# A decode layer on one core: TensorE's program becomes a loop of four turns, K is turned with each head's columns side by side, and w1 is loaded behind wq

## The chip, the core and the metric

The kernel runs on one core of a Trainium2 chip. The core has five engines, each with its own instruction stream: TensorE (matrix products, PE in the profile), VectorE (DVE), ScalarE (ACT), GpSimd (POOL) and SyncE (SP), which here only issues transfers. Sixteen DMA engines move data between the chip's HBM and the on-chip memory SBUF; products land in PSUM. The engines wait for each other by semaphores. The metric is the device time of one execution in microseconds; the median of three runs is given.

## What is computed

One decode step for two sequences (B = 2, one token each): a layer norm of x, then attention over the last 2048 positions of a cache with 8 K/V heads of 256 and 16 query heads, and beside it a small feed-forward gate.

```python
xn = _layernorm(x)                                    # x: 2 x 1 x 448
q  = (xn @ wq).reshape(B, 1, 16, 256)                 # wq: 448 x 4096
k, v = k_cache[:, :, Sk-W:], v_cache[:, :, Sk-W:]     # 2 x 8 x 2048 x 256 each
p  = softmax(einsum("bhqd,bhkd->bhqk", q, repeat(k, 2)) * 256**-0.5)
s  = einsum("bhqk,bhkd->bhqd", p, repeat(v, 2)).reshape(B, 1, 4096) @ wo
g  = silu(relu(xn @ w1) @ w2)                         # w1: 448 x 1792, w2: 1792 x 448
out = x + s * g
```

All tensors are bf16. K and V are 16.8 MB each, wq and wo 3.7 MB each, w1 and w2 1.6 MB each: 44.1 MB are read and 1.8 KB written.

## The kernel before

**Units.** The attention is cut into four units u (`NU`), each of one sequence and four K/V heads: 4 MB of K and 4 MB of V. A transfer lays a unit out with 32 blocks of positions by four heads over the 128 partitions, 64 positions of 256 elements in each. For each unit the following steps run.

- `do_T` (T): VectorE turns K, 32 x 32 words at a time, from `kbuf` into `kt`, in four transposes of 128 x 2048 words. A word is a pair of bf16 elements. There are two `kt` buffers, for even and odd units, and a transpose writes in the order in which it reads.
- `do_S` (S): 32 products of TensorE give the scores, four at a time in four column tiles of the array, one for each head. The moving operand is `kt`, read with a step of 8 elements (16 bytes). The stationary one is a strip of `q_big`, made once for all units by four copies of VectorE behind the turn of q.
- `ch_max`, `ch_spread`, `ch_pt`: VectorE takes the maximum (`mx`, `mxt`, `nbt`, `nb`), ScalarE the exponential with its sum, TensorE spreads the result over the partitions with 16 products and sums, VectorE masks it into `pt` and takes the reciprocal of the sum.
- `do_PV` (PV): 32 products with V as the moving operand, four at a time; ScalarE copies the result to `o_sb`.
- `do_o_pe`, `do_at_exp`, `do_at`: small products and two VectorE steps that lay the unit's result out in `at2`.

**The rest.** Ahead of the units come the layer norm and `do_q`, 28 products against wq. The feed-forward part is `do_h` (first layer, with `do_hn`, `do_hT` and `do_hs`: clamp, turn, copy, on VectorE and TensorE) and `do_F` (second layer, 14 products). At the end come `fold_sums` and `do_gate` for the gate, and 32 blocks of the product with wo, of which the first `WO_TILED` = 24 run in column tiles of the whole width; a copy and four products fold these into one sum, and the other 8, cut in four each, are added to it. Two VectorE steps and a store close the program.

**Order.** Nothing is planned by a machine: `op` and `dma` append to one list per engine, and `run` emits each list as straight code, with a wait in front of an instruction for what it depends on and hasn't yet waited for. So the order in the source from line 466 on is the order on each engine, and a waiting instruction holds everything behind it on its engine. All large transfers are issued by SP in one order: wq, K(0), K(1), V(0), K(2) when T(0) is done, K(3) after T(1), V(1) after PV(0), V(2) after T(2) (into `kbuf[0]`), w1 after S(2) (into a `kt` buffer), V(3) after PV(1), w2, and wo in five parts after T(3).

On TensorE and VectorE the units overlap: T(u+1) lies beside S(u), its last quarter beside the exponential, and the small products of unit u lie between those of unit u+1. The lines that matter most below:

```python
            deps = [d_k[u], st.get(("S", u - 2))] + ([st["q_mm"]] if u == 1 else [])
            st["T", u] = pr.op(DVE, lambda e: e.transpose(
                dst[:, 2048 * c:2048 * c + 2048], src[:, 2048 * c:2048 * c + 2048]), deps)
...
                    o = pr.op(PE, mm(sbk[u % 2][32 * h:32 * h + 8, :], q_big[:, lo:lo + 8],
                                     view(kt[u % 2], 64 * (gp // 2) + gp % 2 + 2 * h, [[256, TS], [8, 8]]),
                                     gp == 0, gp == NG - 1, tile_position=(0, 32 * h)), deps)
```

Every product goes through the helper `mm`, so nearly all of TensorE's work has its line, 187, and the groups are told apart by their tiles: `sp<-kt,q_big` is S, `sp<-e_sb,sel` the spread, `sp<-vbuf,pt` and `sp<-kbuf,pt` are PV, `gbk<-kbuf,at` and `hbk<-kbuf,at` the product with wo. Transposes of K have line 315, all transfers line 37.

Of the kernel before, what the change touches and what calls it, by code (L numbers as in the profile page):

```python
# [15 lines left out]
class _Op:  # L16
    __slots__ = ("eng", "fn", "deps", "dma", "needed", "value", "sem")

    def __init__(self, eng, fn, deps, dma):
        self.eng, self.fn, self.deps, self.dma = eng, fn, deps, dma  # L20
        self.needed, self.value, self.sem = dma, 0, None


class _Prog:


    def __init__(self, nc, es):
        self.nc, self.es = nc, es
        self.lists = {PE: [], DVE: [], ACTE: [], SP: [], POOL: []}

    def op(self, eng, fn, deps=()):
        o = _Op(eng, fn, [d for d in deps if d is not None], False)
        self.lists[eng].append(o)
        return o

    def dma(self, eng, dst, src, deps=()):
        o = _Op(eng, lambda e: e.dma_start(dst, src), [d for d in deps if d is not None], True)
        self.lists[eng].append(o)
        return o

    def run(self):

        nc = self.nc
        n = 0
        for ops in self.lists.values():
            for o in ops:
                for d in o.deps:
                    d.needed = True
        for e, ops in self.lists.items():
            sem, count = self.es.enter_context(self.nc.semaphore(f"s_{e}")), 0  # L50
            for o in ops:
                if o.dma:
                    n += 1
                    o.sem, o.value = self.es.enter_context(self.nc.semaphore(f"d_{n}")), 16
                elif o.needed:
                    count += 1
                    o.sem, o.value = sem, count
        engines = ((POOL, nc.gpsimd), (SP, nc.sync), (ACTE, nc.scalar), (PE, nc.tensor), (DVE, nc.vector))
        for name, eng in engines:
            hint = eng.mark_branch_hint_location() if name == DVE else None  # L60
            self.emit(eng, self.lists[name])
            if hint is not None:
                eng.br("fin").branch_hint(hint)
        nc.switch_bb("fin")

    def emit(self, eng, ops):
        seen = {}
        for o in ops:
# [9 lines left out]
            if o.needed:  # L78
                made.then_inc(o.sem, 16 if o.dma else 1)


def bass_recurrent_scan__sliding_block_cached__dense_activation_relu__decode_kernel(
# [30 lines left out]
    WO_PARTS = [10, 10, 4, 6, 2]  # L113
    WO_TILED = 24

    es = contextlib.ExitStack()
    with es:
# [31 lines left out]
        q_big = named("q_big", [128, NU * NG * 32], BF)  # L149
# [10 lines left out]
        nb = [named(f"nb{i}", [128, 32], F32) for i in range(2)]  # L160
        ssum = [named(f"ssum{i}", [128, 1], F32) for i in range(2)]
        rs = [named(f"rs{i}", [128, 1], F32) for i in range(NU)]
        e_sb = [named(f"e_sb{i}", [128, 512], BF) for i in range(2)]
        pt = [named(f"pt{i}", [128, 512], BF) for i in range(2)]
        fs = named("fs", [128, D], F32)
        o_sb = named("o_sb", [128, 512], BF)
        at_exp = named("at_exp", [128, 64], BF)
# [3 lines left out]
        kt = [named(f"kt{i}", [128, UW], BF) for i in range(2)]  # L171
        wq_sb = kt[1]
        wo_sb = kbuf[1]
        w1_sb = kt[0]
        W2_AT = SLOTS * FC

        sp = psum("sp", [128, 2048], F32)
        sbk = [sp[:, 512 * i:512 * i + 512] for i in range(2)]
# [17 lines left out]

        def unit_src(u, cache):
# [13 lines left out]
        vhome = [vbuf, vbuf, kbuf[0], vbuf]  # L211
        d_k, d_v = {}, {}
# [7 lines left out]
        p_qb = pr.op(POOL, lambda e: e.memset(q_big[:, :].bitcast(F32), 0.0))  # L220
# [6 lines left out]
        a_z = [pr.op(ACTE, lambda e, t=t: e.memzero(t[:, :])) for t in (mbk, gbk, hbk)]  # L227
# [45 lines left out]
        for r in range(1, 4):  # L273
            v_xr = pr.op(DVE, lambda e, r=r: e.tensor_copy(
                view(xr, 32 * r, [[128, SLOTS], [1, 4]]), view(xr, 0, [[128, SLOTS], [1, 4]])), [v_xr])
# [6 lines left out]
        def load_v(u, deps=()):  # L282
            d_v[u] = pr.dma(SP, vhome[u][:, :], unit_src(u, A_v_cache), deps)


        def do_q():
# [19 lines left out]
            for qd in range(4):  # L306
                st["q"] = pr.op(DVE, lambda e, qd=qd: e.tensor_copy(  # L307
                    view(q_big, qd, [[NG * 32, NU], [32, NG], [4, 8]], n=32, p0=32 * qd),
                    view(q_t, 0, [[1, NU], [32, NG], [256, 8]], n=32, p0=32 * qd)), [v, p_qb])


        def do_T(u, c):
            src, dst = kbuf[u % 2][:, :].bitcast(F32), kt[u % 2][:, :].bitcast(F32)
            deps = [d_k[u], st.get(("S", u - 2))] + ([st["q_mm"]] if u == 1 else [])
            st["T", u] = pr.op(DVE, lambda e: e.transpose(  # L315
                dst[:, 2048 * c:2048 * c + 2048], src[:, 2048 * c:2048 * c + 2048]), deps)

        def do_S(u):
            deps = [st["T", u], st["q"], st.get(("exp", u - 2)), *st["q_n"]]
            for gp in range(NG):  # L320
                for h in range(HU):
                    lo = (u * NG + gp) * 32 + 8 * h
                    o = pr.op(PE, mm(sbk[u % 2][32 * h:32 * h + 8, :], q_big[:, lo:lo + 8],
                                     view(kt[u % 2], 64 * (gp // 2) + gp % 2 + 2 * h, [[256, TS], [8, 8]]),
                                     gp == 0, gp == NG - 1, tile_position=(0, 32 * h)), deps)
                    deps = []
            st["S", u] = o


        def ch_max(u):  # L330
            k = u % 2
            v = pr.op(DVE, lambda e: e.tensor_reduce(out=mx[:, 0:1], in_=sbk[k], axis=AX.X, op=ALU.max),  # L332
                      [st["S", u], p_mx, st.get("mxt")])
            v = st["mxt"] = pr.op(DVE, lambda e: e.transpose(mxt[:, :], mx[:, :]), [v, st.get("neg")])  # L334
            v = st["neg"] = pr.op(DVE, lambda e: e.tensor_reduce(
                out=view(nbt, 0, [[4, 2], [1, 4]]), in_=view(mxt, 0, [[4, 2], [0, 4], [1, 4]]),
                axis=AX.X, op=ALU.max, negate=True), [v, p_nbt, st.get("nb")])
            v = st["nb"] = pr.op(DVE, lambda e: e.transpose(nb[k][:, :], nbt[:, :]), [v, st.get(("exp", u - 2))])  # L338
            st["exp", u] = pr.op(ACTE, lambda e: e.activation(  # L339
                e_sb[k][:, :], sbk[k], ACT.Exp,  # L340
                bias=nb[k][:, 0:1], accum_out=ssum[k][:, 0:1]),
                [v, st.get(("spread", u - 2)), st.get(("sum", u - 2))])

        def ch_spread(u):
            deps = [st["exp", u], v_sel, st.get(("pt", u - 1)), *st["q_n"]]
            for i in range(16):
                r, kb = divmod(i, 8)
                o = pr.op(PE, mm(spk[:, TS * r:TS * r + TS], sel[:, 128 * i:128 * i + 128],
                                 view(e_sb[u % 2], kb, [[8, TS]]), i == 0, kb == 7), deps)
                deps = []  # L350
            st["spread", u] = o
            st["sum", u] = pr.op(PE, mm(view(xbk, u, [[1, 1]]), sumsel[:, :], ssum[u % 2][:, 0:1], True, True),
                                 [v_ss, st.get(("r", u - 1))])

        def ch_pt(u):
            st["pt", u] = pr.op(DVE, lambda e: e.tensor_tensor(  # L356
                out=view(pt[u % 2], 0, [[128, 4], [1, 128]]), in0=view(sp, 1024, [[0, 4], [1, 128]]),
                in1=view(hmask, 0, [[1, 4], [0, 128]]), op=ALU.mult),
                [st["spread", u], v_hm, st.get(("PV", u - 2))])
# [221 lines left out]
```

## Time and profile before

| | |
|---|---|
| median of 3 runs | 111.37 us (111.21 to 111.9) |
| profiled execution: its time, its span | 111.33 us, 109.9 us |
| TensorE products, busy | 68.5 us (62% of the span) |
| VectorE, busy | 59.8 us (54%) |
| ScalarE, GpSimd, busy | 12.2 us, 4.4 us |
| mean granted clock of TensorE | 0.81 |
| HBM read | 44.11 MB, 402 GB/s over the span |

The span reaches from the first to the last instruction. In the row PEclk the digits are the clock granted to TensorE in tenths of full speed (9 is 90% or more), in the row DMA the busy share of the sixteen DMA engines, each digit for a fortieth of the span (2.75 us). A line of the groups has the source line, engine, operation, output and inputs, partitions x elements of each and the number of instructions; then the busy time in us and the mean ns of one; then the idle time ahead of them with what ended it.

### The profile page before, as it was taken

To read this page: it belongs to the slowest core of one execution; us is meant where nothing else is said; L and a number is where in the kernel's file an instruction comes from. 1 tells how busy PE (TensorE), PEld (TensorE's weight loads), DVE (VectorE), ACT (ScalarE), POOL (GpSimd) and SP (SyncE) were. 2 spreads that over 40 slices of the span, in tenths; PEclk is the share of its full clock that TensorE was granted. 3 is DMA by queue.
4 is the path that set the end of the run, shared out by engine and by line. 5 is a ranking of instruction groups with operands and counts; after the bars stand their busy time and mean duration, and the time that the engine had idled before them with its cause. 6 is when DMAs were issued, how large, how long until landed. Compare 5 with 4: busy or idle time off the path is not lost.

```text
span 109.9 us, 1131 instructions
## 1 busy us (share of the span) xinstructions
PE 68.5 (62%) x490; PEld 23.3 (21%) x469; DVE 59.8 (54%) x84; ACT 12.2 (11%) x21; POOL 4.4 (4%) x14
## 2 busy tenths in 40 slices
PE   0010699500001995579995699989999892556871
PEld 0000001000000110553110622146213841211330
DVE  2167000399999996825984879995005026003621
ACT  2930000340000000201000200040001300020000
POOL 7800000000000000000000000000000000000000
PEclk9999999995555599656999755999999999955555
DMA  6798998999899989989999999999899998999920
GB/s 168 334 460 388 513 430 382 418 489 430 382 501 441 394 382 525 430 382 406 483 430 394 430 489 406 394 477 447 344 425 496 453 406 363 413 433 417 413 115 1
DMA packets 2463, 44.16 MB, mean 402 GB/s; under 512 B 282, under 2 KB 412, under 8 KB 924
## 3 DMA queue, kind: packets, MB, share of 16 engines
q1 hardware_dynamic: 2432, 44.11, 94.3%
q8 instruction: 3, 0.05, 0.2%
q10 hardware_dynamic: 28, 0.01, 0.0%
HBM read 44.11 MB, written 0.00 MB: 402 GB/s over the span
## 4 chain that ended last, share of the span: by engine, by line
DMA 36%; PE 32%; DVE 26%; issue 2%; ACT 1%; SPq 0%
DMA kbuf<-in_A_wo_dram 26%; PE sp L187 23%; DVE kt L315 15%; DMA kt<-in_A_wq_dram 10%; PE sp L192 6%; DVE q_t L305 2%; DVE mx L332 2%; DVE q_big L307 2%; PE gbk L187 2%; ACT e_sb L339 1%; PE hbk L187 1%; DVE q_n L299 1%; DVE pt L356 1%; DVE mxt L334 1%; DVE nb L338 1%
## 5 line engine op out<-in xcount | busy, mean ns | idle before, releaser
L187 PE MATMUL sp<-kt,q_big 128*8 128x512 bf16 x128 | 30.1, 1088 | 14.4 <-DVE kt L315 14.4
L315 DVE STREAM_TRANSPOSE kt<-kbuf 128x2048 f32<-128x2048 f32 x16 | 35.6, 2274 | 2.8 <-DMA kbuf<-in_A_k_cache_dram 2.7
L187 PEld LDWEIGHTS sp<-kt,q_big 128*8 128x8 bf16 x128 | 4.7, 103 | 34.0 <-issue 18.4
L187 PE MATMUL sp<-e_sb,sel 128*128 128x64 bf16 x64 | 8.1, 294 | 5.3 <-ACT e_sb L339 5.3
L187 PE MATMUL sp<-vbuf,pt 128*16 128x512 bf16 x96 | 8.0, 492 | 2.4 <-DMA vbuf<-in_A_v_cache_dram 1.9
L187 PEld LDWEIGHTS sp<-e_sb,sel 128*128 128x128 bf16 x64 | 7.0, 119 | 8.2 <-ACT e_sb L339 8.2
L339 ACT ACTIVATE e_sb<-sp,nb 128x512 bf16<-128x512 f32 x4 | 2.8, 688 | 51.5 <-DVE nb L338 51.5
L332 DVE TENSOR_REDUCE mx<-sp 128x1 f32<-128x512 f32 x4 | 2.7, 687 | 9.4 <-PE sp L187 9.4
L192 PE MATMUL sp<-kt,xr 128*128 128x512 bf16 x21 | 7.7, 488 | 0.0
L299 DVE TENSOR_SCALAR q_n<-sp 128x1024 bf16<-128x1024 f32 x1 | 1.2, 1225 | 10.5 <-PE sp L192 10.5
L187 PE MATMUL sp<-kt,xr 128*128 128x512 bf16 x7 | 3.6, 512 | 3.7 <-DMA kt<-in_A_wq_dram 3.7
L187 PE MATMUL mbk<-ident,xg 2*128 2x2 bf16 x7 | 0.3, 163 | 7.9 <-DVE xg L237 7.9
L356 DVE TENSOR_TENSOR pt<-sp,hmask 128x512 bf16<-128x512 f32 x4 | 2.8, 698 | 4.2 <-PE sp L187 4.2
L387 DVE TENSOR_TENSOR at_exp<-mbk,qmask 128x64 bf16<-128x64 f32 x4 | 0.8, 204 | 7.2 <-PE mbk L187 7.2
L187 PEld LDWEIGHTS sp<-vbuf,pt 128*16 128x16 bf16 x96 | 3.1, 120 | 7.0 <-DMA vbuf<-in_A_v_cache_dram 3.7
L372 ACT ACTIVATE o_sb<-sp 128x512 bf16<-128x512 f32 x4 | 2.4, 593 | 17.9 <-PE sp L187 17.9
L399 DVE TENSOR_SCALAR at<-mbk,rs 64x32 bf16<-64x32 f32 x4 | 1.4, 350 | 3.6 <-PE mbk L187 3.6
L187 PEld LDWEIGHTS sp<-kt,xr 128*128 128x128 bf16 x7 | 0.8, 121 | 10.7 <-issue 6.9
L187 PE MATMUL gbk<-kbuf,at 128*17 128x448 bf16 x24 | 3.0, 570 | 0.1
L302 ACT ACTIVATE q_n<-sp 128x1024 bf16<-128x1024 f32 x1 | 1.0, 1024 | 14.5 <-PE sp L192 14.5
L187 PE MATMUL gbk<-kt,h_sb 128*17 128x448 bf16 x14 | 1.7, 569 | 1.3 <-DMA kt<-in_B_w_dram 1.3
L305 DVE STREAM_TRANSPOSE q_t<-q_n 128x2048 bf16<-128x2048 bf16 x1 | 2.3, 2311 | 0.0
(74 smaller groups left out, 45.8 us busy)
## 6 DMA issues: line engine op xcount, KB each, us to landing
kbuf<-in_A_k_cache_dram SPq DMA_DIRECT2D x4, 4096.0 KB, 17.9
vbuf<-in_A_v_cache_dram SPq DMA_DIRECT2D x3, 4096.0 KB, 21.6
kbuf<-in_A_v_cache_dram SPq DMA_DIRECT2D x1, 4096.0 KB, 18.7
kt<-in_A_wq_dram SPq DMA_DIRECT2D x1, 3584.0 KB, 11.2
kt<-in_B_w_dram SPq DMA_DIRECT2D x2, 1568.0 KB, 19.3
kbuf<-in_A_wo_dram SPq DMA_DIRECT2D x2, 1120.0 KB, 27.3
kbuf<-in_A_wo_dram SPq DMA_DIRECT2D x1, 672.0 KB, 29.3
kbuf<-in_A_wo_dram SPq DMA_DIRECT2D x1, 448.0 KB, 29.1
```

The lines of the kernel that those rows point to most:

```text
L187: return lambda e: e.matmul(out_ap, lhsT=lhsT, rhs=rhs, start=start, stop=stop, skip_group_check=True, **kw)
L192: return lambda e: e.add_instruction(mybir.InstMatmult(name=nc.get_next_instruction_name(), start_tensor_calc=start, stop_tensor_calc=stop ...
L299: e.tensor_scalar(out=view(q_n, 0, [[64, 16], [32, 2], [1, 32]]), in0=view(sp, 0, [[64, 16], [1, 2], [2, 32]]), scalar1=SCALE, scalar2=Non ...
L305: v = pr.op(DVE, lambda e: e.transpose(q_t[:, :], q_n[:, :]), halves)
L307: st["q"] = pr.op(DVE, lambda e, qd=qd: e.tensor_copy(view(q_big, qd, [[NG * 32, NU], [32, NG], [4, 8]], n=32, p0=32 * qd), view(q_t, 0, [ ...
L315: st["T", u] = pr.op(DVE, lambda e: e.transpose(dst[:, 2048 * c:2048 * c + 2048], src[:, 2048 * c:2048 * c + 2048]), deps)
L332: v = pr.op(DVE, lambda e: e.tensor_reduce(out=mx[:, 0:1], in_=sbk[k], axis=AX.X, op=ALU.max), [st["S", u], p_mx, st.get("mxt")])
L334: v = st["mxt"] = pr.op(DVE, lambda e: e.transpose(mxt[:, :], mx[:, :]), [v, st.get("neg")])
L339: st["exp", u] = pr.op(ACTE, lambda e: e.activation(e_sb[k][:, :], sbk[k], ACT.Exp, bias=nb[k][:, 0:1], accum_out=ssum[k][:, 0:1]), [v, st ...
L356: st["pt", u] = pr.op(DVE, lambda e: e.tensor_tensor(out=view(pt[u % 2], 0, [[128, 4], [1, 128]]), in0=view(sp, 1024, [[0, 4], [1, 128]]), ...
L372: st["osb", u] = pr.op(ACTE, lambda e: e.activation(o_sb[:, :], obk[:, :], ACT.Copy), [o, st.get(("oT", u - 1))])
L399: st["at", u] = st["mbk"] = pr.op(DVE, lambda e: e.tensor_scalar(out=view(at2, 16 * b, [[32, 32]], n=64, p0=p0), in0=mbk[p0:p0 + 64, 32:64 ...
```

## The change

- **TensorE.** Straight code up to the first layer of the feed-forward part, then a loop of four turns, one for each unit, then straight code for the end. A turn is S, (in the last turn: the second layer), spread, PV, the products on `o_sb` and the last small one. The loop waits on semaphores of its own, one per kind of step, against a register that counts the turns (`r`; `v16` for transfers, whose semaphores rise by 16).
- **One buffer of each.** For the loop's addresses to be the same in each turn, `kt`, `pt`, `e_sb`, `nb`, `ssum` and the score bank are single, and V always goes to `vbuf`. T(u+1) waits for S(u).
- **T.** Each transpose now writes its words so that a head's columns lie together: word (b, k, h) goes to h * 2048 + b * 8 + k, so that neighbouring writes are 8 KB apart. S then reads `kt` with a step of 2 elements (4 bytes).
- **The q strips.** `q_big` goes; four ScalarE copies fill `qb` for each unit.
- **Transfers.** w1 follows wq, into `vbuf`; V(0) waits for the first layer's products, V(1) for PV(0), K(3) follows it. V(2) and V(3) come in two halves, each waiting for the half of PV that reads it; w2 lies between them, in wq's place. wo comes last, into `kbuf[0]`, in parts of 10, 12, 6, 2 and 2 blocks for 10, 10, 4, 6 and 2, and 28 blocks are tiled for 24.
- **First layer.** Runs right behind q, with 128 columns of the stationary operand instead of 4 and each loaded once for two products; its clamps and copy go from VectorE to ScalarE.
- **Small steps.** `at_exp` has 128 columns for 64, and its product writes all partitions.

```diff
-    WO_PARTS = [10, 10, 4, 6, 2]
-    WO_TILED = 24
+    WO_PARTS = [10, 12, 6, 2, 2]
+    WO_TILED = 28
...
-        kt = [named(f"kt{i}", [128, UW], BF) for i in range(2)]
-        wq_sb = kt[1]
-        wo_sb = kbuf[1]
-        w1_sb = kt[0]
+        kt = named("kt", [128, UW], BF)
+        wf = named("wf", [128, UW], BF)
+        wq_sb, w2_sb, w1_sb = wf, wf, vbuf
+        wo_sb = kbuf[0]
...
+        def load_v_half(u, k):
+            lo, hi = k * UW // 2, (k + 1) * UW // 2
+            pr.dma(SP, vbuf[:, lo:hi], unit_src(u, A_v_cache)[:, :, lo:hi],
+                   [st["PV" if k else "PVa", u - 1]], kind="VB" if k else "VA")
...
         def do_T(u, c):
-            src, dst = kbuf[u % 2][:, :].bitcast(F32), kt[u % 2][:, :].bitcast(F32)
-            deps = [d_k[u], st.get(("S", u - 2))] + ([st["q_mm"]] if u == 1 else [])
+            src, dst = kbuf[u % 2][:, :].bitcast(F32), kt[:, :].bitcast(F32)
             st["T", u] = pr.op(DVE, lambda e: e.transpose(
-                dst[:, 2048 * c:2048 * c + 2048], src[:, 2048 * c:2048 * c + 2048]), deps)
+                dst.rearrange("p (h b k) -> p b k h", h=HU, k=8)[:, 64 * c:64 * c + 64],
+                src[:, 2048 * c:2048 * c + 2048].rearrange("p (b k h) -> p b k h", k=8, h=HU)), [d_k[u], st.get(("S", u - 1))],
+                kind="T" if c == 3 else None)
...
+        def do_qb(u):
+            for qd in range(4):
+                st["qb", u] = pr.op(ACTE, lambda e, qd=qd: e.activation(
+                    view(qb, qd, [[32, NG], [4, 8]], n=32, p0=32 * qd),
+                    view(q_t, u, [[32, NG], [256, 8]], n=32, p0=32 * qd), ACT.Copy),
+                    [st["q"], p_qb, st.get(("S", u - 1))], kind="QB" if qd == 3 else None)
...
+            with block("turn"):
+                wait("QB", r)
+                wait("T", r)
+                for gp in range(NG):
+                    for h in range(HU):
+                        o = mm(sbk[32 * h:32 * h + 8, :], qb[:, 32 * gp + 8 * h:32 * gp + 8 * h + 8],
+                               view(kt, 4096 * h + 16 * (gp // 2) + gp % 2, [[64, TS], [2, 8]]),
+                               gp == 0, gp == NG - 1, tile_position=(0, 32 * h))(pe)
+                o.then_inc(pr.kinds["S"], 1)
+                pe.br_lt(r, NU, on_true="spread", on_false="second_layer")
+            with block("second_layer"):
+                do_F(pe)
+                pe.br("spread")
+            with block("spread"):
+                hint = pe.mark_branch_hint_location()
+                wait("EXP", r)
...
+                wait("PT", r)
+                for k in range(2):
+                    wait("VB" if k else "VA", v16)
+                    for tp in range(16):
...
+                    o.then_inc(pr.kinds["PV" if k else "PVa"], 1)
+                wait("OSB", r)
+                wait("AT", r)
...
+                wait("AE", r)
+                mm(mbk[:, 32:64], at_exp[:, :], fold[:, :], False, True)(pe).then_inc(pr.kinds["at_mm"], 1)
+                pe.reg_add(r, r, 1)
+                pe.reg_add(v16, v16, 16)
+                pe.br_lt(r, NU + 1, on_true="turn", on_false="tail").branch_hint(hint)
...
+        d_w1 = pr.dma(SP, w1_sb[:, 0:SLOTS * FC], w1_src)
         load_k(0)
         load_k(1)
         do_q()
+        do_h()
...
+        do_qb(0)
         for c in range(4):
             do_T(0, c)
...
+        load_v(0, [st["h", 0], st["h", 1]])
         load_k(2, [st["T", 0]])
...
+        for u in range(NU):
+            ch_max(u)
+            ch_exp(u)
+            if u < NU - 1:
+                do_qb(u + 1)
+                do_T(u + 1, 0)
+            else:
+                copy_sums(st["F"])
+            ch_pt(u)
+            if u < NU - 1:
+                for c in range(1, 4):
+                    do_T(u + 1, c)
+            do_osb(u)
+            do_at_exp(u)
+            do_at(u)
+            if u == 0:
+                load_v(1)
+                load_k(3, [st["T", 1]])
+        load_v_half(2, 0)
+        load_v_half(2, 1)
+        pr.dma(SP, w2_sb[:, 0:14 * D].rearrange("p (hf f) -> p hf f", hf=2), w2_src, [st["q_mm"]], kind="w2")
+        load_v_half(3, 0)
+        load_v_half(3, 1)
...
-            d_wo[j0] = pr.dma(SP, wo_sb[:, j0 * D:(j0 + n) * D], wo_src[:, j0 * D:(j0 + n) * D], [st["T", 3]])
+            d_wo[j0] = pr.dma(SP, wo_sb[:, j0 * D:(j0 + n) * D], wo_src[:, j0 * D:(j0 + n) * D], [st["T", 2]])
```

## The prediction

> **What bounds the kernel now.** I read the page's 40 slices and its read total first, then the chain, then the groups by line.
>
> ```profile
> PEclk9999999995555599656999755999999999955555
> DMA  6798998999899989989999999999899998999920
> HBM read 44.11 MB, written 0.00 MB: 402 GB/s over the span
> ```
>
> The sixteen DMA engines are busy from the second slice to the thirty-eighth (a slice is 2.75 us), whatever the compute engines do. The page's chain says the same of its end: from 75.26 to 103.75 us it is the transfer of wo, and only 6 us follow. So the kernel is a stream of 44.11 MB at some 427 GB/s (44.11 MB over the 103 us in which it runs). As long as compute keeps ahead of the stream it costs nothing; what decides is whether it still does.
>
> VectorE's and TensorE's groups, with the time of one instruction behind the busy time:
>
> ```profile
> L315 DVE STREAM_TRANSPOSE kt<-kbuf 128x2048 f32<-128x2048 f32 x16 | 35.6, 2274 | 2.8 <-DMA kbuf<-in_A_k_cache_dram 2.7
> L187 PE MATMUL sp<-kt,q_big 128*8 128x512 bf16 x128 | 30.1, 1088 | 14.4 <-DVE kt L315 14.4
> L187 PE MATMUL sp<-kbuf,pt 128*16 128x512 bf16 x32 | 1.9, 382 | 0.0
> ```
>
> Both matmul groups run four at a time. Reading kt in steps of 16 bytes, 32 of them (one unit's scores, S) take 7.50 us; reading V in one run, 32 take 1.93 us, or 3.62 us in the first unit, where the clock was halved (48.00 to 51.62). Four transposes (T, one unit's turn of K) follow one another every 2.22 us: 26.35 to 35.25. Today T of the next unit lies beside S of this one, because kt has two buffers.
>
> **The change, part by part.**
>
> *One kt buffer.* T(u+1) now waits for S(u), and S(u+1) for T(u+1): they add up instead of overlapping. This makes the cost of each decide.
>
> *S.* [...] The reductions on VectorE show what steps cost on a read: one run, 8-byte steps, 64-byte steps.
>
> ```profile
> L246 DVE TENSOR_REDUCE qmask<-ident 128x4 f32<-128x128 bf16 x1 | 0.3, 276 | 0.0
> L253 DVE TENSOR_REDUCE hmask<-ident 128x4 f32<-128x128 bf16 x1 | 0.3, 274 | 0.0
> L251 DVE TENSOR_REDUCE fold<-ident 128x32 bf16<-128x128 bf16 x1 | 0.4, 353 | 0.0
> ```
>
> Steps of 8 bytes are free, so I price S like PV's one run: 1.93 us at full clock, 3.62 at half. Bound above: 7.50 as now. Which clock? TensorE is idle for some 6 us before each S.
>
> ```profile
> 37.00:38.00 1.00, 1.00 (x11) 0.17 (x7) 1.00 (x2) 0.00 (x0) 0.00 (x0) 0.54 0.91 393
> 38.00:39.00 1.00, 1.00 (x12) 0.25 (x8) 1.00 (x1) 0.00 (x0) 0.00 (x0) 1.00 1.06 459
> ```
>
> In these windows (the third number from the right is the granted clock) S(0), begun at 35.29, got the full clock only 2.7 us in. I take 3.62.
>
> *T.* Each transpose now writes its elements 8 KB apart: four heads, then back to the neighbouring word. No row shows such a 4-byte write. From below: free, 2.22 us. From above, the isolated 2-byte writes of the kernel, against one that writes short runs:
>
> ```profile
> L270 DVE TENSOR_TENSOR xr<-mbk,par 128x28 bf16<-128x28 f32 x1 | 0.2, 178 | 0.0
> L432 DVE CAST h_sb<-hbk 128x28 bf16<-128x28 f32 x1 | 0.3, 285 | 0.6 <-PE hbk L187 0.6
> L399 DVE TENSOR_SCALAR at<-mbk,rs 64x32 bf16<-64x32 f32 x4 | 1.4, 350 | 3.6 <-PE mbk L187 3.6
> ```
>
> (285 - 178)/28 is 3.8 ns more for each write, the other row some 5.3; at 3.8, T would take 2.22 + 2048 x 0.0038 = 10 us. [...] Nearest in order is L251: it too visits four places 64 bytes apart and returns to the neighbour of the first; (353 - 276)/128 = 0.60 ns an element, though on a read. I take it: T every 2.22 + 1.23 = 3.45 us. This is the weakest number here, and it counts sixteen times.
>
> [...]
>
> *Start.* w1 (1.6 MB) goes ahead of K(0): 1.6/0.427 = 3.8 us later for everything behind it. K(2) landed at 50.65 (T(2) waited for it) with 20.4 MB in the queue up to it; 9.5 MB are now queued up to K(0), so it lands at 50.65 - 10.9/0.427, about 25.1. T(0) began at 26.35 behind the four copies into q_big (1.82 us), which go to ScalarE; so it begins at 25.2 instead, 1.1 earlier. The first layer (h) runs behind q on TensorE (2.8 us, 87.7 to 90.5 now) from 20.9, its clamps and the q copies on ScalarE; done by about 28, beside T(0). If that cover went, 3 us would be added once.
>
> *SP's queue.* V(0) waits for h (24), K(2) for T(0), V(1) for PV(0), K(3) behind V(1) for T(1), V(2) and V(3) in halves for PV, wo behind all for PV(2). If compute keeps up, each wait ends before the queue is dry (PV(0) 48.5 against some 52, PV(2) 86 against 90.8), and the stream stays whole. The extra issues (three, 0.54 us each) hide behind transfers of 4.9 us. If compute is late the stream has gaps, which cost nothing while compute is later still.
>
> *A turn,* from one S to the next: S 3.62; max to nb 1.44 (42.82 to 44.26); first transpose 3.45, which covers exponential and spread (0.79 + 2.1); pt and reciprocal 0.79; three transposes 10.35; at_exp, its matmul and hand-overs 0.52. PV (3.62, V landed in time), o_sb and its matmuls (0.9) lie beside the three transposes, and are the next thing late if those shrink: 6.66 at the old price still cover them. Sum 20.17.
>
> *The sum.* T(0) ends 25.2 + 13.8 = 39.0; S(3) starts at 39.0 + 3 x 20.17 = 99.5. Last turn: S 3.62, second layer 1.7 (98.46 to 100.1 now), spread 2.1, pt 0.8, PV 1.93 (TensorE has been busy 7 us, so full clock), o_sb 0.62, then 0.27, 0.23, 0.25, 0.4 as now: 111.4. wo has landed by then (PV(2) begins at 88.6, its halves free V's at 90.4 and 92.2; two halves of 4.9 us and wo's 8.6 follow, to about 111). The end: 28 tiled wo products 1.5 (half as fast at half clock), copy 0.68, fold 0.33, sixteen products 0.5 (thirty-two took 0.97), the last two VectorE steps 0.64, store 1.74 (108.16 to 109.9): 116.8. Around the span lie 111.33 - 109.9 = 1.43 us; this execution stands at the median (111.37). That gives 118.2; register, branch and wait instructions of the loop, a few tenths a turn that no row prices (below: nothing), I put at 0.8 in all. **119.0 us.**
>
> Its own range: with T at 3.1 instead of 3.45, 16 x 0.35 = 5.6 less; with PV and wo at half clock 3.3 more, and T at 3.7 four more: 113.5 to 126.
>
> **Rivals.**
>
> *A, scattered writes are free (0.22).* Then T(0) ends at 34.1, S(3) follows T(3), PV(3) follows V's last half at 97.7, and the end is the wo stream again. For it: the transposes keep 1.04 ns an element, and the copies into q_big step 512 bytes at 443 ns for 256. Price: the tail. wo's last tiled piece ends 0.46 MB later in the stream (1.07 us), has six products for four (+0.12), sixteen untiled fewer (-0.47): +0.6, so 111.9, not slower by more than 1%. It decides below a T of about 3.0, where the chain (16 us for each 1 us of T) falls under the stream.
>
> *B, scattered writes are dearer.* At two cycles an element (2.08 ns), T is 4.36 and the sum 16 x 0.91 = 14.6 more: 133.6 (0.08). At the 3.8 ns of L432 it is 7.8 - 1.2 = 6.6 more sixteen times, 224 (0.06).
>
> *C, S is not faster.* The 4-byte step is no run; at 7.50 us, four times 3.9 more: 134.5 (0.06). Against it speaks L253.
>
> *D, the branch back refetches.* The jump stands between one turn's last matmul and the next S. The shortest transfer of the trace, x_sb, took 1.34 us from issue to use (0.74 to 2.08); if each of three jumps costs that, 4 more: 123.0 (0.08). For it: today's program has no jump in TensorE. [...]
>
> **The numbers.** Forecast 0.50. Within 1% is what a measurement of this kernel can hardly tell from no change (its runs span 0.6%). A gives 0.04 faster, 0.16 same, 0.02 slower; of the forecast 0.04 falls to same and 0.01 to faster where T is near 3.0. So faster 0.05, same 0.20, slower 0.75. The range 110.6 to 130 holds A, the forecast and D, some 0.8 of the chance; B and C lie above it.
>
> **What would show it.** The mean of the transpose group: 3.5 us (forecast), 2.27 (A), 4.4 or 10 (B). S per unit: 3.6 or less, else 7.5. DMA slices well below 9 after the half if compute is late; all 9 if A. The chain: transposes and S in turns to the end, not wo. An idle stretch on TensorE ahead of each S with T already done would be D. The forecast is wrong first of all if a read's price does not carry over to a write.

## The result, and the profile after

The changed kernel takes **124.05 us** (median of 4 runs, 123.08 to 124.84) where the kernel before, run beside it, takes 111.29 (110.88 to 111.9): a ratio of 1.114 [1.102, 1.125]. The forecast was 119.0 with a range of 110.6 to 130.0. Here and below, ratios and intervals are taken from runs within 1.5% of the fastest run of the same kernel; where there are too few of them, all runs are listed.

The profiled execution took 123.08 us, with a span of 120.7. Its granted clock, its DMA slices (3.02 us each), its read total and the shares of its chain of waits:

```profile
PEclk9999999995555555555555555555555555596898
DMA  5998989898989999999898989999902799999300
HBM read 44.11 MB, written 0.00 MB: 365 GB/s over the span
DVE 47%; DMA 20%; PE 18%; issue 11%; ACT 1%; SPq 1%
```

The same 44.11 MB are read, but the stream is no longer whole. In slices 30 and 31 it is all but dry (no more was asked for until PV(2), which starts at 90.12 us, had read half of V(2)), and it is over well before the end. VectorE and TensorE now take turns as the bound. The groups by line show what their instructions cost (the last column is idle time ahead of them and what ended it):

```profile
L351 DVE STREAM_TRANSPOSE kt<-kbuf 128x2048 f32<-128x2048 f32 x16 | 57.5, 3684 | 1.0 <-DMA kbuf<-in_A_k_cache_dram 1.0
L221 PE MATMUL sp<-kt,qb 128*8 128x512 bf16 x128 | 14.3, 623 | 15.7 <-DVE kt L351 14.9
L221 PE MATMUL sp<-vbuf,pt 128*16 128x512 bf16 x128 | 14.1, 618 | 3.7 <-DVE pt L380 3.7
L221 PE MATMUL mbk<-fold,at_exp 128*128 128x32 bf16 x4 | 0.8, 203 | 19.2 <-DVE at_exp L392 19.2
```

A transpose went from 2274 to 3684 ns, a product of S from 1088 to 623, much the same as one of PV at this clock (618). The 14.9 us of waiting for transposes are a single wait, ahead of S(0) (14.4 before). In the turns TensorE's wait is put down to `at_exp`, which stands behind the three transposes in VectorE's list: 19.2 us in all. One turn in the chain of waits (start, duration, what; short pieces of "issue" between VectorE's small steps are left out):

```profile
60.29 3.61 PE sp L221 x25
...
63.92 0.70 DVE mx L365
...
65.25 3.70 DVE kt L351
68.95 0.52 DVE pt L380
...
69.54 4.64 DVE kt L351 x2
74.19 2.38 issue
76.57 3.64 DVE kt L351
80.22 0.13 DVE at_exp L392
...
80.39 0.21 PE mbk L221
80.60 0.27 issue
80.87 3.61 PE sp L221 x32
```

(The 4.64 us and the 2.38 of "issue" behind them are the second and third transpose, 7.0 us, whose ends the view doesn't show in one piece.) Every piece of the turn hangs on the one before; nothing overlaps T with S. The turns start at 39.68, 60.29, 80.87 and 101.45 us: 20.6 us from one to the next, three times; the last turn has no transposes.

The two executions of the changed kernel that have a trace differ in the clock granted in the last turn: where PV(3) took 3.27 us and the tiled wo products 1.50 (0.50 granted at 110 to 112 us, 0.71 up to 113.5, 1.00 up to 117), the run took 123.08; where they took 3.64 and 2.61 (the repeat below, 0.50 granted from 108 to 115 us), 124.27. Whether this sets the level of the other runs isn't shown.

### The profile page after: what moved, and what is told of

Its sections match the earlier page's. It is cut to its first block, busy times and chain, and to the rows that moved or that the text cites. A ratio compares the mean times of both kernels' runs of the same rounds, so it can differ in the third digit from the quotient of the medians.

```text
span 120.7 us, 1159 instructions
## 1 busy us (share of the span) xinstructions
PE 55.6 (46%) x478; PEld 22.0 (18%) x450; DVE 78.1 (65%) x77; ACT 18.6 (15%) x40; POOL 4.3 (4%) x15
## 2 busy tenths in 40 slices
DMA packets 2748, 44.11 MB, mean 365 GB/s; under 512 B 314, under 2 KB 572, under 8 KB 956
## 3 DMA queue, kind: packets, MB, share of 16 engines
q1 hardware_dynamic: 2720, 44.11, 86.7%
HBM read 44.11 MB, written 0.00 MB: 365 GB/s over the span
## 4 chain that ended last, share of the span: by engine, by line
DVE 47%; DMA 20%; PE 18%; issue 11%; ACT 1%; SPq 1%
DVE kt L351 39%; DMA kbuf<-in_A_k_cache_dram 20%; PE sp L221 16%; DVE mx L365 2%; DVE pt L380 2%; PE mbk L221 1%; PE hbk L221 1%; DVE mxt L367 1%; DVE tmp L512 1%; DVE nbt L371 1%; SPq L52 1%; DVE at_exp L392 1%; ACT o_sb L388 1%; DVE fs L490 0%; DVE nb L374 0%
## 5 line engine op out<-in xcount | busy, mean ns | idle before, releaser
L351 DVE STREAM_TRANSPOSE kt<-kbuf 128x2048 f32<-128x2048 f32 x16 | 57.5, 3684 | 1.0 <-DMA kbuf<-in_A_k_cache_dram 1.0
L221 PE MATMUL sp<-kt,qb 128*8 128x512 bf16 x128 | 14.3, 623 | 15.7 <-DVE kt L351 14.9
L221 PE MATMUL sp<-vbuf,pt 128*16 128x512 bf16 x128 | 14.1, 618 | 3.7 <-DVE pt L380 3.7
L221 PE MATMUL mbk<-fold,at_exp 128*128 128x32 bf16 x4 | 0.8, 203 | 19.2 <-DVE at_exp L392 19.2
L221 PEld LDWEIGHTS sp<-kt,qb 128*8 128x8 bf16 x128 | 3.9, 115 | 22.9 <-issue 22.9
L226 PE MATMUL sp<-wf,xr 128*128 128x512 bf16 x21 | 7.7, 488 | 0.0
L221 PEld LDWEIGHTS sp<-vbuf,pt 128*16 128x16 bf16 x128 | 4.2, 134 | 10.7 <-issue 6.6
L358 ACT ACTIVATE qb<-q_t 32x64 bf16<-32x64 bf16 x16 | 5.5, 344 | 0.1
L221 PE MATMUL sp<-wf,xr 128*128 128x512 bf16 x7 | 3.6, 509 | 3.6 <-DMA wf<-in_A_wq_dram 3.6
L392 DVE TENSOR_TENSOR at_exp<-mbk,qmask 128x128 bf16<-128x128 f32 x4 | 1.1, 277 | 4.2 <-PE mbk L221 4.2
L342 ACT ACTIVATE q_n<-sp 128x1024 bf16<-128x1024 f32 x1 | 1.0, 1023 | 14.4 <-PE sp L226 14.4
L221 PEld LDWEIGHTS sp<-wf,xr 128*128 128x128 bf16 x7 | 0.9, 122 | 10.6 <-issue 6.9
L221 PE MATMUL gbk<-vbuf,xr 128*128 128x448 bf16 x7 | 2.5, 353 | 0.0
## 6 DMA issues: line engine op xcount, KB each, us to landing
vbuf<-in_B_w_dram SPq DMA_DIRECT2D x1, 1568.0 KB, 14.4
```

Source lines behind the costliest of these rows:

```text
L221: return lambda e: e.matmul(out_ap, lhsT=lhsT, rhs=rhs, start=start, stop=stop, skip_group_check=True, **kw)
L226: return lambda e: e.add_instruction(mybir.InstMatmult(name=nc.get_next_instruction_name(), start_tensor_calc=start, stop_tensor_calc=stop ...
L351: st["T", u] = pr.op(DVE, lambda e: e.transpose(dst.rearrange("p (h b k) -> p b k h", h=HU, k=8)[:, 64 * c:64 * c + 64], src[:, 2048 * c:2 ...
L358: st["qb", u] = pr.op(ACTE, lambda e, qd=qd: e.activation(view(qb, qd, [[32, NG], [4, 8]], n=32, p0=32 * qd), view(q_t, u, [[32, NG], [256 ...
L392: st["at_exp", u] = pr.op(DVE, lambda e: e.tensor_tensor(out=view(at_exp, 0, [[64, 2], [4, 16], [1, 4]]), in0=view(mbk, 0, [[0, 2], [1, 16 ...
```

## The experiments

Three questions were open: whether the price of T is one of hopping and what a hop is; how the loss divides between the layout of `kt` and the rest, the single buffer above all; and what the loop, the place of w1 and the time outside the span have to do with it. "Before" is the kernel before on the same chip, 111.0 to 111.3 us each time.

### The changed kernel again

> The changed kernel once more, beside the others on one chip, so that they have something to be compared with. Expected: 123 to 125 us, transposes at 3.68 us, S at 3.6 us a unit, 20.6 us from one S to the next.

Measured: 124.77 us (124.27 to 124.83), ratio 1.120 [1.113, 1.127]. The transpose took 3679 ns, turns 20.46 to 20.49 us. The loss and its place repeat.

### Pairs of words for single words

The heads are kept in two pairs; T writes two adjacent words, then hops, and S reads in steps of 8 bytes for 4.

```diff
-    dst.rearrange("p (h b k) -> p b k h", h=HU, k=8)
+    dst.rearrange("p (hh b k hl) -> p b k hh hl", hh=2, k=8, hl=2)
...
-    view(kt, 4096 * h + 16 * (gp // 2) + gp % 2, [[64, TS], [2, 8]])
+    view(kt, 8192 * (h // 2) + 2 * (h % 2) + 32 * (gp // 2) + gp % 2, [[128, TS], [4, 8]])
```

> The changed kernel, with T writing two neighbouring words at each place instead of one (heads in two pairs; a head's columns then lie 8 bytes apart), and S reading in steps of 8 bytes instead of 4. Theory (the single-word hop makes a transpose 1.4 us dearer, sixteen times on the one chain): transposes back at 2.27 us; S at 3.6 to 4.4 us; a turn 15 to 16 us; the chain then falls behind the stream of transfers and the end is wo again: span 110 to 111, 111.5 to 113 us. Rival 1 (one kt buffer, that is S and T in series, makes the loss whatever T costs): no less than 117. Rival 2 (any write 8 KB or more away is dear, pairs or not): transposes stay above 3 us, 119 or more.

Measured: 112.7 us (111.89 to 112.94), ratio 1.012 [1.006, 1.018]. Its DMA slices, chain, transposes and S:

```profile
DMA  6798999899899989998999889979999999999950
DMA 75%; PE 19%; SPq 1%; DVE 1%; issue 1%
L351 DVE STREAM_TRANSPOSE kt<-kbuf 128x2048 f32<-128x2048 f32 x16 | 35.7, 2276 | 1.6 <-DMA kbuf<-in_A_k_cache_dram 1.6
L221 PE MATMUL sp<-kt,qb 128*8 128x512 bf16 x128 | 15.9, 652 | 11.1 <-DVE kt L351 10.2
```

This is the decisive run. One buffer, loop, order of transfers and everything else are those of the changed kernel; only the hop is halved in number, and the transpose is back at 2276 ns (2274 before). At the clocks granted here S pays little for the wider step (652 against 623), but it no longer gains from a full clock: in S(0) the median product took 650 ns while half the clock was granted (34.36 to 36.40 us) and 651 with all of it (36.50 to 38.34; the clock row has 5 in slice 13 and 8 in slice 14, which ends at 38.26 us). At steps of 4 bytes a product follows the clock: in the run with two buffers below it falls from 632 ns to 401 within S(1), when the full clock comes (5 in slice 21 of the clock row, 9 in slice 22), and with w1 behind K(0) the products of S take from 392 to 632 ns. The stream is whole and sets the end, as before, with a span of 109.3 us (109.9 before). The price of T is that of a 4-byte word which stands alone (3684 ns for 2276 with pairs), and 12.1 of the 13.6 us lost hang on it as long as S stays cheap too (124.77 less 112.70, beside 111.19 before, all on one chip).

### A near hop

The four heads lie 32 bytes apart in a block of 128 bytes, for 8 KB apart; S still reads in steps of 4 bytes.

```diff
-    dst.rearrange("p (h b k) -> p b k h", h=HU, k=8)
+    dst.rearrange("p (b h k) -> p b k h", h=HU, k=8)
...
-    view(kt, 4096 * h + 16 * (gp // 2) + gp % 2, [[64, TS], [2, 8]])
+    view(kt, 64 * (gp // 2) + gp % 2 + 16 * h, [[256, TS], [2, 8]])
```

> The changed kernel with T writing single words that hop 32 bytes, inside a block of 128 bytes, where the changed kernel hops 8 KB; a head's eight columns of a block still lie side by side, so S reads in steps of 4 bytes as there. It tells what the price hangs on. If on the distance (8 KB), transposes come back to 2.3 us. If on the hop alone, they stay at 3.7. [...] My own guess from the reductions over steps of 64 bytes (0.60 ns more an element): 3.5 to 3.7.

Measured (one profiled run): 126.54 us.

```profile
L351 DVE STREAM_TRANSPOSE kt<-kbuf 128x2048 f32<-128x2048 f32 x16 | 59.1, 3782 | 2.1 <-DMA kbuf<-in_A_k_cache_dram 2.1
```

3782 ns against 3684: between these two distances it is not the distance that costs, but the step away from the neighbouring word. The near hop is a little the dearer one: from one transpose to the next it is 3.68 us for 2048 columns, 1.80 ns a column, for 3.55 us and 1.73 ns with the far one.

### The new layout alone, with two buffers

The kernel before, with T's and S's patterns of the changed kernel and nothing else: no loop, two `kt`, its own order of transfers.

```diff
-    dst[:, 2048 * c:2048 * c + 2048], src[:, 2048 * c:2048 * c + 2048]), deps)
+    dst.rearrange("p (h b k) -> p b k h", h=HU, k=8)[:, 64 * c:64 * c + 64],
+    src[:, 2048 * c:2048 * c + 2048].rearrange("p (b k h) -> p b k h", k=8, h=HU)), deps)
...
-    view(kt[u % 2], 64 * (gp // 2) + gp % 2 + 2 * h, [[256, TS], [8, 8]])
+    view(kt[u % 2], 4096 * h + 16 * (gp // 2) + gp % 2, [[64, TS], [2, 8]])
```

> The kernel before with the new layout alone: T writes single words 8 KB apart, S reads in steps of 4 bytes; two kt buffers, straight program, old order of transfers. Theory (the price of T is the loss, with or without the second buffer): transposes 3.68 us, S 2 to 3.6 us a unit; T(u+1) runs beside S(u), but K(2), K(3) and V(1) to V(3) are issued later by what T is late, and the stream gets gaps of some 8 us; 117 to 121 us. Rival (the single buffer is the loss, T is hidden by the second one): 113 or less.

Measured: 119.50 us (118.95 to 120.25; a fourth run took 121.11), ratio 1.076 [1.067, 1.085].

```profile
DMA  6999999989899488950499898989989898899940
DVE 57%; DMA 28%; PE 10%; issue 3%; SPq 0%
L315 DVE STREAM_TRANSPOSE kt<-kbuf 128x2048 f32<-128x2048 f32 x16 | 57.9, 3710 | 0.0
```

So the layout alone makes a kernel slower that overlaps T with S. VectorE never waits ahead of a transpose (0.0): from 26.45 us on it is the bound, and the transfers that wait for it leave holes in the stream: the 4, and then the 5, 0 and 4 in the slices, which end where SP may issue K(2) and K(3), behind T(0) (40.63 us) and T(1) (56.15). The chain of waits goes by transposes up to 89.53 us, where the issue of wo follows the last of them, and then by 22 us of transfer. The single buffer is not needed for a loss; with the rest of the change it makes it larger, by some 4 to 5 us.

### The new structure alone, with the old layout

The changed kernel, with T writing as it reads and S reading in steps of 16 bytes.

```diff
-    dst.rearrange("p (h b k) -> p b k h", h=HU, k=8)[:, 64 * c:64 * c + 64],
+    dst[:, 2048 * c:2048 * c + 2048],
...
-    view(kt, 4096 * h + 16 * (gp // 2) + gp % 2, [[64, TS], [2, 8]])
+    view(kt, 64 * (gp // 2) + gp % 2 + 2 * h, [[256, TS], [8, 8]])
```

> The changed kernel with the layout of the kernel before: T writes in the order in which it reads, S reads in steps of 16 bytes. Everything else (loop, one buffer of each, order of transfers) as changed. Theory: transposes 2.27 us, S 7.5 us a unit; T(0) ends 5.3 us earlier; a turn is 3.9 longer for S and 4.6 to 4.8 shorter for T, so some 20.0; last turn 3.9 longer: 5.3 + 2 - 3.9 = 3.4 less than the changed kernel, 120 to 121 us. So the new layout by itself is a small loss within the new structure, and neither layout brings the structure back to 111. Rival (the layout alone is the loss): 113 or less.

Measured: 118.84, 121.01, 121.61 and 121.82 us, without an interval; what sets the fastest apart isn't known, as it has no trace. In the profiled one (121.61, span 119.3):

```profile
L221 PE MATMUL sp<-kt,qb 128*8 128x512 bf16 x128 | 30.2, 1090 | 10.6 <-DVE kt L351 9.7
L351 DVE STREAM_TRANSPOSE kt<-kbuf 128x2048 f32<-128x2048 f32 x16 | 35.7, 2275 | 1.1 <-DMA kbuf<-in_A_k_cache_dram 1.1
```

S is 7.51 us again, T is cheap, and the turn is 19.96 us (S starts at 34.48, 54.42, 74.38 and 94.38) against 20.58. So turn by turn the two layouts come out nearly even with one buffer: 3.9 us a turn that S gains with the new layout, T gives back, 4.2 in the last three transposes (10.68 us for 6.52) and 0.7 in the first, where with the old layout the exponential and the spread set the time; VectorE's small steps take 0.3 less. Over the whole kernel the old layout is 2.2 to 5.2 us below the 124.05 of the new one. And each half of the change loses by itself, the layout 8.5 us (119.50), the structure 7.6 to 10.6: the two do not add up to the 12.8 of both, and only where T and S are cheap at once, as with the pairs, is the chain short enough for the stream.

### No loop

TensorE's program written out straight, waiting on constants.

```diff
-            with block("turn"):
+            for u in range(NU):
+                r, v16 = u + 1, 16 * (u + 1)
                 wait("QB", r)
...
-                pe.reg_add(r, r, 1)
-                pe.reg_add(v16, v16, 16)
-                pe.br_lt(r, NU + 1, on_true="turn", on_false="tail").branch_hint(hint)
```

> The changed kernel with the four turns written out one behind the other: no turn register, no jumps, waits on constants; everything else as it is. The trace shows 0.22 us more at each jump between the last product of a turn and S than a hand-over takes, and 2.35 us outside the span where the kernel before has 1.43. Theory (the loop itself costs little): 0.66 us less in the span. If what lies outside the span is the loop's too, 0.9 less on top: 122.4 us in all where the changed kernel takes 124.0; if not, 123.3. Rival (the loop is a main cause): 115 or less.

Measured: 120.4 and 120.76 us in two runs, 124.78 and 138.08 in the other two, which have no trace that says why; no interval can be given. In the profiled one (120.76) S follows the last small product of the turn before at once, where the loop shows 0.27 us of "issue", and the turns are 20.25 us long against 20.58. So a jump costs 0.27 us, 0.8 in all; the rest of the turn's difference is S (3.54 for 3.61). What is left of the difference to 123.08 is mostly the clock of the last turn: S(3) took 3.11 us for 3.61 and PV(3), which had it full (1.00 in the windows from 109 to 112 us), 1.96 for 3.27, while T(0) began 0.65 us later. The outside of the span is 2.36 us, as with the loop.

The same was tried with pairs of words (the two edits together):

> The pairs of words of e1_pairs in the program without the loop (e2_unroll). With pairs the end is the stream of transfers, so the 0.2 us that each jump takes should be hidden: within 0.3 us of e1_pairs, 112.7. If the jumps held the stream back, 112 or less. Its span should be that of the kernel before (109.3 to 110), and what lies outside the span 2.3 us or more, as in all kernels built on the changed program, against 1.5 before.

Measured: 113.52 us (113.02 to 113.77), ratio 1.021 [1.016, 1.026]; without the loop it is 0.8 us slower than with it, where 0.3 at most was expected. The spans lie further apart, 110.7 to 111.4 us for 109.3 to 110.3, because the runs with the loop had up to 3.44 us outside theirs. (The two ran on different chips.) The transposes are the same (2277 ns). What hangs on the stream is later: the first product against wq starts at 12.35 us for 11.85, those against wo's last tiled piece at 106.18 for 105.07. The straight program fetches instructions through a DMA queue (0.07 MB more of DMA traffic in the page's total, 44.18 for 44.11), the loop's page shows no such queue. Whether that is the cause wasn't tested; the kernel before fetches 0.05 MB in this way too, and its first product against wq starts at 11.96.

### w1 behind K(0)

The changed kernel with two transfers exchanged.

```diff
-        d_w1 = pr.dma(SP, w1_sb[:, 0:SLOTS * FC], w1_src)
         load_k(0)
+        d_w1 = pr.dma(SP, w1_sb[:, 0:SLOTS * FC], w1_src)
         load_k(1)
```

> The changed kernel with w1's transfer put behind K(0), ahead of K(1): its start alone. Theory (the chain from the first transpose on is what lasts, and all that starts it later is added whole): K(0) lands some 3.8 us sooner, so that T(0) waits for the copies of the first layer, the turn of q and VectorE's own list instead and begins at about 24.4 for 25.4; later turns as they were: about 1 us less than the changed kernel, 123 to 124 beside 124.0 to 124.8. Rival (a start is made up later, the stream ends last): the same time as the changed kernel. If w1 behind K(0) delays V(0), which waits for the first layer, PV(0) is late and the gain is gone.

Measured: 122.92 us (121.95 to 123.35), ratio 1.102 [1.097, 1.108]: 1.1 us below the changed kernel. The chain of waits no longer has a transfer of K in it:

```profile
21.19 1.24 DVE q_n L339
22.42 0.02 issue
22.45 0.07 DVE q_t L345
22.52 2.16 issue
24.68 14.20 DVE kt L351 x4
```

T(0) begins at 24.68 us, behind the turn of q, for 25.36 behind K(0). S is also a little shorter here (3.3 to 3.46 us for 3.61), so the 1.1 us are not the start's alone. Beside the execution of 124.27 us, whose PV(3) took 3.64 us as here, the profiled run (123.04) is 1.2 us shorter: T(0) begins 0.85 us sooner and the four S together take 0.4 less. What starts the chain later is added to the end: w1's place costs 0.7 to 0.85 us now that the chain, and not the stream, is last.

### Pairs in the kernel before

The best of the new layouts in the old structure, as a candidate that might be faster than both.

```diff
-    dst[:, 2048 * c:2048 * c + 2048], src[:, 2048 * c:2048 * c + 2048]), deps)
+    dst.rearrange("p (hh b k hl) -> p b k hh hl", hh=2, k=8, hl=2)[:, 64 * c:64 * c + 64],
+    src[:, 2048 * c:2048 * c + 2048].rearrange("p (b k hh hl) -> p b k hh hl", k=8, hh=2, hl=2)), deps)
...
-    view(kt[u % 2], 64 * (gp // 2) + gp % 2 + 2 * h, [[256, TS], [8, 8]])
+    view(kt[u % 2], 8192 * (h // 2) + 2 * (h % 2) + 32 * (gp // 2) + gp % 2, [[128, TS], [4, 8]])
```

> The kernel before (no loop, two kt buffers, its order of transfers), with one edit: T writes pairs of adjacent words, heads in two pairs, and S reads steps of 8 bytes. Theory (a pair of words pays no hop; S at 8-byte steps runs with the clock; all of it lies beside the stream, which is whole): T 2.28 us, S some 2 to 3.6 us for a unit in place of 7.5, and the time that of the kernel before within 0.5%: 110.8 to 111.9. Rival (S was on the path, and its gain shows): 110 or less. Rival (the pairs cost something that the one-buffer kernel hid): T above 2.4 and 112 or more.

Measured: 111.19 us (110.64 to 112.25, 12 runs), ratio 1.000 [0.997, 1.003].

```profile
DMA  7799999999999999999999899999899997999940
L187 PE MATMUL sp<-kt,q_big 128*8 128x512 bf16 x128 | 15.8, 649 | 14.4 <-DVE kt L315 14.4
```

TensorE's work on S is halved, 14 us of it gone, and the time doesn't move: the stream sets it. This is what S was worth in the kernel before. No kernel tried here is faster than it.

### What lies outside the span

The changed kernel has 2.30 to 2.38 us outside its span, the kernel before 1.43 to 1.53 in most runs and up to 2.5 in a few: 0.9 us that the forecast didn't have. All kernels of the new structure have 2.3 or more in every run, with the loop or without, with any layout; the old structure with the new layout alone has 1.50 to 3.01. Two counts in which the structures differ were changed in the kernel before. The first gives each step of ScalarE a semaphore of its own (38 in all, for 24; the changed kernel has 39), the second cuts each transfer of V in halves (23 transfers for 19; the changed kernel has 21).

```diff
+                elif o.needed and e == ACTE:
+                    n += 1
+                    o.sem, o.value = self.es.enter_context(self.nc.semaphore(f"a_{n}")), 1
```

> The kernel before, where each ScalarE instruction that is waited for has a semaphore of its own: 38 semaphores instead of 24 (the changed kernel has 39). All instructions and transfers as before. All kernels built on the changed program, with the loop or without, take 0.8 us or more outside the span beyond the kernel before's 1.5. If that is the number of semaphores, this one shows it too: 0.8 us more, 112.0, with the same span. If not, 111.2.

```diff
-            d_v[u] = pr.dma(SP, vhome[u][:, :], unit_src(u, A_v_cache), deps)
+            d_v[u] = [pr.dma(SP, vhome[u][:, k * UW // 2:(k + 1) * UW // 2],
+                             unit_src(u, A_v_cache)[:, :, k * UW // 2:(k + 1) * UW // 2], deps) for k in range(2)]
```

> The kernel before with each transfer of V cut in two halves, both issued where the one was: 23 transfers for 19 (the changed kernel has 21), nothing else. It asks where the 0.9 us outside the span come from (2.3 to 2.4 in the changed kernel, 1.43 to 1.5 before). Theory (each transfer more costs time outside the span): 2.3 or more outside, 112 to 113. Rival (the number of transfers is not it): 1.43 to 1.5 outside and the time of the kernel before, 110.8 to 112; then it stays open.

Measured: 111.33 us, ratio 1.002 [0.999, 1.005], and 111.25 us, ratio 1.002 [1.000, 1.004]; outside the span 1.43 to 1.53 us in most runs of both. Neither count alone brings the 2.3, and the cause stays open.

## Why the prediction was right, and where it was off

The direction and the mechanism held, at every place where the prediction named what would show them: the chain of waits goes by transposes and S in turns to the end, the mean of a transpose is 3.68 us, nearest the 3.5 of the forecast, S is 3.6, and the DMA slices have a hole late. The time came out 5 us above the number, inside the range. By the steps, in the profiled execution (forecast 119.0, measured 123.08):

| step | forecast | measured | to the end |
|---|---|---|---|
| T(0) begins | 25.2 | 25.36 | +0.2 |
| T, from one to the next, in T(0) | 3.45 | 3.55 | +0.4 |
| S | 3.62 | 3.61 | 0 |
| a turn: max to nb | 1.44 | 1.35 | -0.1 |
| first T, to pt | 3.45 | 3.70 | +0.25 |
| pt and reciprocal | 0.79 | 0.59 | -0.2 |
| three T | 10.35 | 10.68 | +0.3 |
| at_exp, its product, hand-over and jump | 0.52 | 0.65 | +0.15 |
| the turn | 20.17 | 20.58 | three times +0.4 |
| from S(3) to the end of the last turn's at | 11.9 | 13.9 | +2.0 |
| from there to the end of the span | 5.4 | 5.4 | 0 |
| loop instructions, in all | 0.8 | in the turns | -0.8 |
| outside the span | 1.43 | 2.38 | +0.95 |

With S(0) behind T(0) 0.1 us later than written, the last column adds up to the 4.1 us.

**T.** The weakest number was right to 3%: 0.60 ns an element, taken from L251, a read that hops 64 bytes, stands for a write that hops 8 KB. That it fits so closely is in part luck: it comes from another operation, on half words, and no run compares the price of a read with that of a write. The rows that gave 10 us (half words, each alone) were rightly thought too far. The trace has 3.55 us from one transpose to the next in T(0), 1.73 ns a column, where the row gave 3.45 and 1.68.

**S and its clock.** S at 4-byte steps runs like PV's one run, at the halved clock: 3.61 us. The row of the clock has 5 from slice 10 to slice 35; in the repeat it has some higher digits there (6 to 9), and S took 3.49. That the idle stretch ahead of S is the reason, as the forecast had it, was not tested, and the next step speaks against so simple a rule.

**The last turn, the step that failed.** It took 2.0 us more than its sum, by two terms. PV(3) was put at 1.93 us "so full clock", because TensorE would have been busy for 7 us. It took 3.27 us here, and 3.64 in the run of 124.27 us. In windows of the last turn (from and to, length, busy us of TensorE, weight loads, VectorE, ScalarE and GpSimd, granted clock, DMA share, GB/s), from the end of S(3) over the second layer and the spread (107.36 to 109.38) to PV(3):

```profile
105.00:107.00 2.00, 1.36 (x18) 0.29 (x6) 1.81 (x5) 0.47 (x1) 0.00 (x0) 0.74 1.04 437
107.00:109.00 2.00, 1.64 (x15) 1.65 (x16) 0.03 (x1) 0.30 (x2) 0.00 (x0) 1.00 1.01 430
109.00:110.00 1.00, 0.49 (x6) 0.40 (x3) 0.60 (x1) 0.00 (x0) 0.00 (x0) 0.73 0.90 382
110.00:111.00 1.00, 0.85 (x12) 0.31 (x16) 0.17 (x2) 0.00 (x0) 0.00 (x0) 0.50 1.04 430
111.00:112.00 1.00, 1.00 (x16) 0.44 (x12) 0.00 (x0) 0.00 (x0) 0.00 (x0) 0.50 0.97 384
```

and PV(3) in the straight program:

```profile
110.00:111.00 1.00, 1.00 (x24) 0.47 (x16) 0.00 (x0) 0.00 (x0) 0.00 (x0) 1.00 1.00 414
```

The full clock was there for the spread, as forecast (1.00 at 107 to 109 us), but it was taken back as PV(3) came up (0.50 at 110 to 112). If it is either half or full, a share of 0.74 puts its beginning at 106.04 us and one of 0.73 its end at 109.46: an estimate of 3.4 us. In this stretch TensorE ended the second layer (106.35), was idle for 1.0 us and ran the spread. In the straight program it stayed (1.00 from 105 to 112 us), and PV(3) took 1.96 us; so the forecast was one of two cases. What grants the full clock and takes it back was not shown: that 7 us of work bring it was the author's estimate, and no run moved these steps against the clock on purpose. The term is 1.3 us of the 4.1. In the run of 124.27 us the half clock (0.50 from 108 to 115 us, 6 in slice 39 of the clock row) also holds through the tiled wo products (2.61 us for 1.50), which makes its 1.2 us more.

The other term is what lies between S(3) and the spread. The sum has the second layer there, 1.7 us; but the spread waits for the maximum and the exponential, which run on VectorE and ScalarE beside it and which the turn's own terms put at 1.44 + 0.79 = 2.23 us. They took 2.27 (105.09 to 107.36). That is 0.6 us more.

**The end.** The gate (g_sb, behind exp and two steps of VectorE) ends at 117.21, and the copy of wo's sum, which stands behind it in VectorE's list, starts there:

```profile
115.50 0.27 ACT ea L509
...
115.80 0.23 DVE ea L510
...
116.05 0.86 DVE tmp L512
...
116.94 0.27 DVE g_sb L513
117.21 0.54 DVE fs L490
```

The sum had the copy right behind the wo products. These begin at 115.39 and are busy for 1.50 us, so that the gate cost some 0.3 us; shorter steps behind it (the copy 0.54 us for 0.68, fold and last products 0.60 for 0.83) made up for it. Where the half clock makes them end at 118.29, in the run of 124.27 us, it cost nothing.

**Outside the span.** 0.95 us, taken over from the kernel before as a constant. This is the share of the miss that no view of the span explains.

**The rivals.** A, free writes, is excluded by the transposes, and what it describes was built with the pairs: 112.7 us, forecast for A 111.9, and the 0.8 between them is the outside again. B's two cycles an element (4.36 us) and its 10 us are excluded, C's 7.5 us for S too. (That its 1.04 ns is one cycle no run shows; (2311 - 212)/2016 ns lies between two transposes of the kernel before, L334's of 32 columns and L305's of 2048.) D, a refetch at each jump (1.3 us each), is excluded at that price: 0.27 us of "issue" stand ahead of S with T done, none without the loop. That a jump refetches at all was not shown. The 0.8 us put down for the loop in all were right: 3 x 0.27.

**The start.** K(0) landed about when it was said (T(0) begins at 25.36, forecast 25.2), and the cover of the first layer held. But it was counted as a gain of 1.1 us over the kernel before, while T(0) could have started at 24.68 with w1 one place later.

## What to carry to other kernels

Where a transpose on VectorE writes 4-byte words one by one to scattered places, keep two words together: here the hop cost 1.4 us for 2048 words (3684 ns for 2274), and pairs cost nothing (2276), while the reader paid some 5% for the wider step at half clock (652 ns for 623). At full clock it would pay more: 651 ns a product at 8 bytes, 392 to 401 at 4. Before making the reader's access cheaper at the writer's expense, see whether the reader is late at all: halving S moved nothing where the stream set the end. And price the last turn of a chain for both clocks; full speed behind 7 us of work held in one program and not in its twin (PV(3) 1.96 and 3.27 us).

## What the runs showed of the hardware that was not expected

- The distance of a hop hardly matters to a transpose's writes here: 8 KB 3684 ns, 32 bytes within 128 bytes 3782 ns, pairs of words 2276 ns, one run 2275 ns.
- S pays 1088 to 1090 ns a product at a step of 16 bytes, 649 to 652 at 8 bytes and 585 to 624 at 4 bytes, at the clocks that each run was granted; 623 stands beside 618 for V's one run in the same execution. Only the 4-byte step follows the clock: 8 bytes take 650 ns at half clock and 651 at full in one S, 4 bytes 632 and 401.
- The full clock came for an estimated 3.4 us and went again just ahead of the 32 products that needed it (1.00 at 107 to 109 us, 0.50 at 110 to 112), in one execution and not in another of nearly the same program.
- A taken jump of TensorE costs 0.27 us here, with no fetch of instructions in the queues' table (a single packet of 0.02 MB in the run with the near hop); the straight program with pairs fetched 0.07 MB and was 0.8 us slower, not faster.
- 0.9 us more outside the span come with the new structure in every run, and neither the number of semaphores nor that of transfers alone brings them.
